# A DeltaNet and feed-forward kernel: the last 891 steps of a written-out order, arranged anew

## The chip, the cores and the metric

The kernel runs on one core of one Trainium2 chip. The metric is the time of one execution on the device in microseconds (us), the median of several runs.

## The reference

Two blocks stand one behind the other. The first goes through 768 tokens for each of 4 batches and 8 heads and carries a 48 x 48 state:

```python
k_n = k / (np.linalg.norm(k, axis=-1, keepdims=True) + 1e-06)
state = np.zeros((B, H, D, D), dtype=np.float32)
for t in range(S):
    kt, vt, bt = (k_n[:, :, t], v[:, :, t], beta[:, :, t, None])
    y[:, :, t] = np.einsum('bhd,bhde->bhe', q[:, :, t], state)
    v_old = np.einsum('bhde,bhd->bhe', state, kt)
    state = state + bt[:, :, :, None] * np.einsum('bhd,bhe->bhde', kt, vt - v_old)
```

The second takes the heads side by side as 3072 tokens of 384 features:

```python
a = x @ w1
b = x @ w2
h = a * b @ w3
return (h @ w_out).astype(np.float32)
```

w1 and w2 are 384 x 1024, w3 is 1024 x 1024, w_out is 1024 x 384, all in float32.

## The kernel before

The tokens are cut into 12 chunks of 64 (numbered m or c), and two chunks make a pair (j or u, 0 to 5). The token-by-token recurrence is replaced, in each chunk, by products of small matrices, for which a triangular matrix has to be inverted. The feed-forward block works on a pair of chunks at a time; w3 and w_out are first multiplied with each other into w34, and the last product is done with seven half-size products in place of eight (Winograd's form of Strassen).

Each part of the work is a Python generator, and each `yield` ends a step. `ORDER` names 1371 steps; a name stands in it once for each step of its generator, so the third "s4" is the third step of scores(4). The loop below runs them, and `in_text_order` ties every instruction to the one before it on its engine: the order of the text is the order on every engine's queue.

```python
    def step(name):
        if name not in running:
            running[name] = parts[name]()
        next(running[name], None)

    for name in ORDER.split():
        step(name)
    in_text_order()
```

In this document a name with a point, such as s4.0, means the first step of s4. The names that matter here:

- k, v, p: loads of one chunk (k: 4 DMAs on SP, v: 2, p: 8 in each of 2 steps, into `perm`); d: four VectorE transposes of `perm` into `KQ`.
- g (squares) and N (norms): lengths of the keys of a pair: POOL squares (L272), VectorE sums (L274), a tiny TensorE product (L257); N.0 is 15 small VectorE operations.
- s (scores): twice a TensorE step of 48 matmul instructions (L369, L375) and two VectorE steps that read its bank. u: 4 DMAs that carry the result to DRAM.
- V (inverse): loads a pair's triangles as 32 x 32 blocks and inverts them in 31 VectorE steps of a product and a subtraction (L442, L449), each needing the one before; then a DMA stores them. For the first two pairs V works in a PSUM bank.
- e (corner): 8 DMAs load the inverse, VectorE transposes it (L485), and two TensorE steps of 64 matmul instructions (L502) with ScalarE copies behind them (L518, L529) fill in the corner of the 64 x 64 inverse.
- n: POOL scales v. c (chain): three TensorE steps of 64 (L555), each followed by VectorE (R L588, X L598, the state S L619). y (outputs): one TensorE step of 128 (L656), ScalarE copies into `xT` (L677), and for odd chunks 6 DMAs within `xT`.
- P, C, t, f: weights loaded, converted (ScalarE L717, VectorE L722, POOL L724), transposed and folded into w34. C30 to C35 make w2s. T: sums of the folded weight on POOL (L840).
- a and b (ab): for pair u and slice jc, a product with w1s (6 matmul instructions, L791), a ScalarE copy (L803), a product with w2s (6, L791), and a VectorE product of the two (L807). The b steps are the first chunk of pair 0.
- S: 16 POOL sums of slabs (L860); o: seven products of 16 matmul instructions (L888); x (result): ScalarE and VectorE read the banks and SP stores the results.

PSUM is two tiles of two banks ("w", for s, e, c, y) and four banks ("f", for a, b, o, g, N), both given out in turn, so a TensorE step can wait until another engine has read what its bank held. A float32 matmul of the source is two matmul instructions in the profile. TensorE's own queue holds 8444 matmuls, as many weight loads, and 169 semaphore and drain instructions.

Of the kernel before, what the change touches and what calls it, by code (L numbers as in the profile page):

```python
# [52 lines left out]
f7 V1 V1 y0 b2 C31 b2 b5 V1 V1 P17 b3 V1 V1 V1 V1 V1 V1 V1 b5 b4 V1 V1 V1 c1 b6 V1 b6 y1 a05 b3  # L53
V1 V1 C31 V1 V1 C31 V1 b4 a01 a01 V1 V1 V1 a00 V1 V1 a05 a00 V1 V1 V1 C34 P16 V1 a06 b0 b7 a06
V1 b0 V1 V1 V1 V1 C32 C33 b7 p4 b1 V1 V1 V1 V1 C32 a07 V1 V1 a07 C34 a04 V1 V1 V1 V1 a04 V1 V1
V1 V1 V1 V1 V1 V1 V1 a02 V1 V1 k4 g2 V1 V1 b1 a03 d4 d4 a03 C32 C34 a00 b0 C33 C35 a02 a00 v3
k5 b1 n3 C35 b0 b1 a03 a03 g2 g2 b2 b2 g2 a01 C35 V1 b3 v2 c1 a01 C33 b3 b6 a07 n2 V1 b6 V1 g2
g2 p4 a06 g2 c2 g2 g2 d4 d4 e2 e2 e2 a04 e2 n2 a07 c2 a06 e2 s4 e2 T b4 g2 N2 s4 c2 s4 T a02 c2
c2 c2 y2 b4 p5 y2 b5 d5 s4 a04 e3 S0 V2 d5 a05 a02 o0 T N2 e3 n3 c3 a05 s4 s4 b5 T c3 S0 e3 p5
d5 d5 b7 b7 u4 e3 S0 S0 S0 S0 e3 s5 S0 k6 N2 x0 o0 S0 s5 e3 s5 s5 s5 u5 s5 c3 g3 o0 g3 c3 x0 y3  # L60
S0 y3 S0 g3 o0 o0 g3 V2 V2 x0 V2 c3 x0 V2 S0 S0 V2 V2 o0 V2 y3 V2 p6 x0 V2 S0 x0 S0 S0 V2 x0 x0
S0 V2 V2 V2 a10 a10 V2 v4 x0 o0 x0 x0 V2 d6 V2 d6 V2 a12 p6 V2 V2 a13 V2 V2 a12 a13 v5 V2 V2 V2
a14 a11 V2 V2 a17 a17 a14 k7 V2 g3 a14 n4 V2 V2 V2 V2 V2 a14 a17 a11 g3 g3 g3 V2 a13 a13 e4 d6
d6 a11 c3 a16 c4 n4 e4 e4 a17 a11 p7 c4 a16 a15 e4 g3 e4 e4 g3 e5 a15 a15 N3 s6 s6 s6 c4 e5 a12
c4 y4 d7 d7 a15 p7 a16 n5 n5 y4 a12 a16 c4 e5 c4 a10 a10 e5 S1 e5 e5 c5 o1 c5 S1 S1 k8 d7 x1 S1
S1 d7 s7 s7 s7 s7 S1 s7 s7 S1 S1 g4 g4 o1 v6 g4 s6 s6 s6 S1 u7 c5 o1 V3 c5 x1 y5 c5 u6 g4 V3 S1
c5 V3 V3 y5 x1 o1 o1 S1 S1 y5 c6 V3 S1 V3 p8 S1 n6 x1 S1 V3 V3 V3 V3 V3 o1 x1 V3 x1 S1 x1 a20
a20 o1 n6 V3 x1 V3 V3 V3 V3 a24 a24 x1 x1 a25 V3 a25 V3 a22 V3 V3 d8 k9 d8 V3 V3 V3 V3 a21 p8
a27 a27 a21 V3 V3 V3 V3 x1 V3 V3 a27 a22 V3 V3 v7 n7 V3 g4 e6 a20 a27 e7 d8 a23 d8 a23 g4 a24
a26 g4 g4 a20 a24 c6 N3 p9 n7 g4 S2 e6 g4 e6 a26 a26 N4 e6 s8 s8 e6 a25 N3 e7 e6 s8 a26 c6 c6  # L70
s8 N4 s8 s8 N4 y6 y6 d9 d9 e7 e7 a23 a21 a25 a23 c6 u8 c6 e7 p9 d9 a22 d9 V4 a22 e7 a21 S2 S2
s9 s9 c7 o2 s9 s9 S2 S2 c7 c7 s9 s9 S2 S2 c7 v8 S2 k10 o2 u9 g5 g5 V4 V4 S2 S2 x2 o2 x2 y7 o2
o2 V4 V4 V4 V4 y7 x2 S2 V4 c7 x2 V4 S2 V4 V4 S2 S2 y7 V4 o2 x2 x2 x2 x2 S2 a35 V4 V4 S2 V4 n8
V4 n8 V4 a35 x2 o2 x2 a37 V4 V4 V4 p10 x2 V4 V4 d10 a33 a33 d10 g5 V4 a34 a37 V4 g5 a30 a34 k11
a30 a36 V4 V4 p10 v9 a36 V4 a34 V4 V4 V4 a31 V4 a33 a30 V4 g5 V4 V4 e8 g5 a31 g5 g5 a33 a34 d10
a32 a32 e8 g5 e8 a30 V5 c7 a31 e8 e8 c8 a36 e8 e9 g5 e9 a31 d10 n9 c8 v11 c8 e9 p11 a37 c8 e9
e9 e9 c8 c8 N5 a36 a35 y8 n9 c9 d11 y8 a32 c9 c9 N5 a32 s10 a37 o3 a35 x3 o3 s10 d11 o3 c9 S3
s10 s10 s10 S3 p11 d11 d11 S3 x3 S3 S3 y9 y9 S3 S3 o3 S3 v10 s10 N5 s11 S3 s11 s11 S3 s11 S3 S3
x3 s11 o3 x3 u10 y9 u11 c9 s11 c9 o3 a47 x3 S3 S3 V5 x3 S3 n10 x3 x3 V5 S3 o3 V5 x3 x3 V5 V5 V5
a47 V5 V5 V5 V5 V5 V5 V5 a43 V5 a42 a43 a46 a46 V5 V5 a42 V5 a46 a40 x3 V5 n11 V5 a41 n11 V5 V5  # L80
a46 V5 V5 V5 a41 a40 V5 V5 V5 a47 a41 V5 V5 V5 a45 V5 V5 V5 a47 e10 a41 a40 a45 a44 e10 a43 a45
n10 e11 a40 c10 a43 a44 a45 e10 a44 c10 e10 e10 e11 e10 a42 a42 c10 o4 a44 S4 S4 S4 c10 e11 x4
S4 S4 c10 S4 e11 o4 S4 e11 c10 c11 S4 o4 c11 e11 c11 S4 c11 S4 y10 S4 y10 S4 y11 S4 x4 S4 o4 o4
y11 x4 x4 o4 x4 x4 y11 x4 a50 x4 x4 a50 S4 S4 o4 x4 a50 a55 a55 a50 a55 a51 a57 a51 a55 a51 a51
a54 a54 a56 a57 a52 a52 a52 a53 a56 a53 a56 a53 a52 a54 a57 a54 x4 a56 S5 S5 S5 a53 o5 a57 o5
S5 S5 x5 o5 x5 S5 S5 S5 S5 S5 o5 o5 S5 S5 x5 o5 S5 x5 S5 x5 S5 S5 o5 x5 x5 x5 x5 x5 x5 x5 x5 x5
"""


# [975 lines left out]
```

## Time and profile before

| | |
|---|---|
| median of 3 runs | 600.25 us (599.49 to 600.57) |
| the profiled execution | 601.93 us, span of its instructions 600.2 us |
| mean granted TensorE clock | 0.980 |
| TensorE busy | 542.4 us |
| VectorE, ScalarE, POOL busy | 329.7, 164.2, 173.6 us |
| DMA | 56.54 MB, mean 94 GB/s |

"Granted clock" is the share of TensorE's full clock. In the rows of the trace a wait stands in brackets with what ended it; "issue" means that the engine waited for nothing that the profile shows.

### The profile page before, as it was taken

The page shows a single profiled execution, that of the slowest core. Times are in us where ns is not written, and L with a number is a line of the kernel's source. Part 1 is how long each engine was busy: PE and PEld are TensorE (multiplying, and loading weights), DVE is VectorE, ACT ScalarE, POOL GpSimd, SP SyncE. Part 2 cuts the span into 40 slices and gives each one's busy share as a digit, 9 for nine tenths or more (in the row PEclk, how much of TensorE's full clock was granted, in tenths as well). Part 3 has the DMA queues.
Part 4 walks back from the last instruction along what each step waited for, and adds up shares of the span by engine and source line. Part 5 has one row for each costly group of instructions (what it writes and reads, how often), then busy time and mean ns, then how long its engine had stood idle before and what let it go on. Part 6 is the DMA issues. An engine that isn't in the chain of part 4 may idle for free.

```text
span 600.2 us, 19394 instructions
## 1 busy us (share of the span) xinstructions
PE 542.4 (90%) x8444; PEld 378.7 (63%) x8444; DVE 329.7 (55%) x788; ACT 164.2 (27%) x345; POOL 173.6 (29%) x222
## 2 busy tenths in 40 slices
PE   2378994889899999999999899999999999999997
PEld 2364663658678884558854569645588446884477
DVE  2457763457786379665696644975545963211012
ACT  3486653734312211131211312012310111320100
POOL 6364433230535700207203016021071001500051
PEclk9988996899999999999999989999999999999999
DMA  8959887596953356525546352463253021010001
GB/s 225 219 135 276 233 163 128 82 176 96 164 80 55 56 123 108 98 42 84 103 78 127 50 81 73 82 114 65 40 86 94 14 59 32 5 54 13 1 0 53
DMA packets 204404, 56.54 MB, mean 94 GB/s; under 512 B 193344, under 2 KB 199488, under 8 KB 202528
## 3 DMA queue, kind: packets, MB, share of 16 engines
q1 hardware_dynamic: 200128, 54.52, 46.4%
q10 hardware_dynamic: 4192, 0.79, 0.9%
q8 instruction: 66, 1.08, 0.8%
q14 instruction: 18, 0.15, 0.1%
HBM read 43.09 MB, written 11.01 MB: 90 GB/s over the span
## 4 chain that ended last, share of the span: by engine, by line
PE 80%; DMA 6%; issue 4%; DVE 4%; ACT 4%; SPq 1%; POOL 0%; ACTq 0%; DVEq 0%
PE ps_f L791 39%; PE ps_f L888 18%; PE ps_w L555 5%; PE ps_f L771 5%; PE ps_w L656 4%; DMA raw<-in_moe_w_dram 3%; PE ps_w L502 3%; PE ps_w L369 2%; PE ps_w L375 2%; DMA ktok<-in_k_dram 2%; DVE ps_w L449 1%; DVE tb L442 1%; DMA Vd<-Vb 1%; ACT raw L720 1%; PE ps_w L888 1%
## 5 line engine op out<-in xcount | busy, mean ns | idle before, releaser
L791 PE MATMUL ps_f<-xT,w2s 128*128 128x512 f32 (+1 forms) x336 | 134.2, 544 | 3.0 <-POOL w2s L724 2.8
L860 POOL TENSOR_TENSOR ab<-ab 128x256 f32<-128x256 f32 x96 | 66.8, 728 | 223.5 <-DVE ab L807 190.0
L791 PE MATMUL ps_f<-xT,w1s 128*128 128x512 f32 (+1 forms) x336 | 128.2, 532 | 0.3 <-issue 0.3
L791 PEld LDWEIGHTS ps_f<-xT,w2s 128*128 128x128 f32 x336 | 62.5, 191 | 57.9 <-issue 50.9
L791 PEld LDWEIGHTS ps_f<-xT,w1s 128*128 128x128 f32 x336 | 63.3, 190 | 55.8 <-issue 51.7
L803 ACT COPY ab<-ps_f 128x512 f32<-128x512 f32 (+1 forms) x56 | 27.9, 527 | 185.6 <-PE ps_f L791 185.6
L888 PE MATMUL ps_f<-w,ab 128*128 128x192 f32 x376 | 66.3, 330 | 0.0
L807 DVE TENSOR_TENSOR ab<-ab,ps_f 128x512 f32<-128x512 f32 (+1 forms) x56 | 32.9, 604 | 59.1 <-PE ps_f L791 58.5
L888 PEld LDWEIGHTS ps_f<-w,ab 128*128 128x128 f32 x376 | 61.2, 190 | 3.9 <-issue 2.7
L442 DVE TENSOR_TENSOR tb<-Vb,Ub 128x31 f32<-128x31 f32 (+15 forms) x124 | 43.9, 354 | 16.4 <-DMA Ub<-Ud 13.0
L771 PE MATMUL ps_f<-w2s,w3T 128*128 128x384 f32 x128 | 45.4, 507 | 4.9 <-ACT w3T L765 3.5
L888 PE MATMUL ps_f<-room,ab 128*128 128x192 f32 x272 | 48.0, 330 | 0.8 <-DVE room L919 0.8
L449 DVE TENSOR_TENSOR Vb<-Vb,tb 128x31 f32<-128x31 f32 (+15 forms) x124 | 44.6, 360 | 4.3
L888 PEld LDWEIGHTS ps_f<-room,ab 128*128 128x128 f32 x272 | 44.1, 190 | 1.6 <-issue 1.1
L677 ACT COPY xT<-ps_w 48x256 f32<-48x256 f32 x96 | 30.5, 366 | 49.1 <-PE ps_w L656 48.6
L272 POOL TENSOR_TENSOR sq<-ktok 128x384 f32<-128x384 f32 x24 | 20.2, 852 | 75.7 <-DVE tb L442 39.1
L381 DVE TENSOR_TENSOR U<-ps_w,wt 128x512 f32<-128x512 f32 x24 | 16.5, 689 | 42.6 <-PE ps_w L375 42.5
L771 PEld LDWEIGHTS ps_f<-w2s,w3T 128*128 128x128 f32 x128 | 24.2, 195 | 21.5 <-ACT w3T L765 4.0
L375 PE MATMUL ps_w<-KQ 48*64 48x64 f32 x768 | 29.4, 227 | 6.3 <-issue 4.7
L724 POOL TENSOR_TENSOR w<-w,raw 128x512 uint32<-128x512 uint32 x16 | 20.7, 1298 | 33.1 <-DVE w L722 15.7
L375 PEld LDWEIGHTS ps_w<-KQ 48*64 48x64 f32 x768 | 26.1, 140 | 5.6 <-issue 3.9
L541 POOL TENSOR_TENSOR vtok<-vtok,n 128x384 f32<-128x384 f32 x24 | 19.8, 838 | 33.3 <-DMA vtok<-in_v_dram 33.3
(104 smaller groups left out, 644.7 us busy)
## 6 DMA issues: line engine op xcount, KB each, us to landing
raw<-in_moe_w_dram SPq DMA_DIRECT2D x8, 1024.0 KB, 8.1
vtok<-in_v_dram SPq DMA_DIRECT2D x24, 192.0 KB, 4.5
raw<-in_moe_w_dram SPq DMA_DIRECT2D x12, 384.0 KB, 6.7
out_dram<-osb SPq DMA_DIRECT2D x46, 96.0 KB, 2.7
ktok<-in_k_dram SPq DMA_DIRECT2D x44, 96.0 KB, 3.5
raw<-in_moe_w_out_dram SPq DMA_DIRECT2D x4, 768.0 KB, 5.0
Ud<-U SPq DMA_DIRECT2D x48, 64.0 KB, 2.3
Ub<-Ud SPq DMA_DIRECT2D x6, 512.0 KB, 3.9
```

The lines of the kernel that those rows point to most:

```text
L375: pe.matmul(ps[half(z ^ j), 1, n + C * j : n + C * j + C], lhsT=x[:, 0, :], rhs=x[:, j, :], start=True, stop=True,)
L442: dve.tensor_tensor(out=tv, in0=V[:, 0 : s + 1, s : s + 1].to_broadcast([P, s + 1, n]), in1=U[:, s, s + 1 : BS].unsqueeze(1).to_broadcast( ...
L449: dve.tensor_tensor(out=o, in0=o, in1=tv, op=ALU.subtract)
L555: pe.matmul(out(ps, r, h, z), lhsT=lhs(r, h, z), rhs=rhs(r, h, z), start=True, stop=True,)
L656: i = pe.matmul(region(h, z, r), lhsT=lhs, rhs=rhs, start=part[n] not in part[:n], stop=part[n] not in part[n + 1 :],)
L677: act.copy(out=xT[f, p:NP:2, b : b + NR, cc, :].rearrange("p a r t -> p r a t"), in_=pyv[f, z, b : b + NR],)
L771: pe.matmul(ps[:, 0:DM], lhsT=w3Ts[jc, kc // 4][:, kc % 4 * P : kc % 4 * P + P], rhs=wo[:, kc], start=(kc == 0), stop=(kc == KF - 1),)
L791: pe.matmul(ps[:].rearrange("p b c t -> p b (c t)"), lhsT=w[:, m, js], rhs=x[:, m, :, c0:c1].rearrange("p b c t -> p b (c t)"), start=(m = ...
L803: act.copy(out=t, in_=ps)
L807: dve.tensor_tensor(out=t, in0=t, in1=ps, op=ALU.mult)
L860: pool.tensor_tensor(out=o_, in0=x_, in1=y_, op=op)
L888: pe.matmul(ps[b][:, b, :], lhsT=abs_[u, HF * f + i][:, t0 : t0 + P], rhs=ws_[w][:, i], start=first and i == 0 and (b == 0 or n == "F"), s ...
```

## The change

The first 480 steps keep their places. The 891 that follow are put in a new order, laid out with the exact places where TensorE's packets of instructions begin; no step is added or removed, and no other line of the kernel changes. In the profile TensorE is at 155 us, and VectorE and POOL at about 156 us, where the new order begins. The diff, cut to the places that the text speaks of:

```diff
-V1 V1 V1 V1 V1 V1 V1 a02 V1 V1 k4 g2 V1 V1 b1 a03 d4 d4 a03 C32 C34 a00 b0 C33 C35 a02 a00 v3
-k5 b1 n3 C35 b0 b1 a03 a03 g2 g2 b2 b2 g2 a01 C35 V1 b3 v2 c1 a01 C33 b3 b6 a07 n2 V1 b6 V1 g2
-g2 p4 a06 g2 c2 g2 g2 d4 d4 e2 e2 e2 a04 e2 n2 a07 c2 a06 e2 s4 e2 T b4 g2 N2 s4 c2 s4 T a02 c2
...
-S0 y3 S0 g3 o0 o0 g3 V2 V2 x0 V2 c3 x0 V2 S0 S0 V2 V2 o0 V2 y3 V2 p6 x0 V2 S0 x0 S0 S0 V2 x0 x0
-S0 V2 V2 V2 a10 a10 V2 v4 x0 o0 x0 x0 V2 d6 V2 d6 V2 a12 p6 V2 V2 a13 V2 V2 a12 a13 v5 V2 V2 V2
...
-s8 N4 s8 s8 N4 y6 y6 d9 d9 e7 e7 a23 a21 a25 a23 c6 u8 c6 e7 p9 d9 a22 d9 V4 a22 e7 a21 S2 S2
-s9 s9 c7 o2 s9 s9 S2 S2 c7 c7 s9 s9 S2 S2 c7 v8 S2 k10 o2 u9 g5 g5 V4 V4 S2 S2 x2 o2 x2 y7 o2
-o2 V4 V4 V4 V4 y7 x2 S2 V4 c7 x2 V4 S2 V4 V4 S2 S2 y7 V4 o2 x2 x2 x2 x2 S2 a35 V4 V4 S2 V4 n8
...
-S4 S4 c10 S4 e11 o4 S4 e11 c10 c11 S4 o4 c11 e11 c11 S4 c11 S4 y10 S4 y10 S4 y11 S4 x4 S4 o4 o4
-y11 x4 x4 o4 x4 x4 y11 x4 a50 x4 x4 a50 S4 S4 o4 x4 a50 a55 a55 a50 a55 a51 a57 a51 a55 a51 a51
...
+V1 V1 V1 V1 V1 V1 V1 a02 V1 V1 k4 v2 b1 C34 C32 V1 g2 d4 b1 V1 V1 C33 a03 k5 v3 b3 a02 b1 n2 n2
+a00 a00 a02 d4 V1 C35 C35 V1 a03 p4 b3 a01 g2 C33 a02 C35 b5 c1 b5 a01 a03 a07 e2 b6 g2 g2 g2
+g2 a06 b6 e3 a03 g2 g2 c2 n3 e2 e2 c2 a07 b4 a06 e2 e2 e2 T b4 a04 g2 c2 d4 d4 p5 g2 a04 c2 b0
...
+S0 S0 x0 S0 o0 S0 S0 s5 V2 V2 y3 x0 o0 c3 V2 V2 g3 x0 V2 y3 y3 V2 V2 V2 k7 S0 o0 x0 x0 V2 x0 x0
+x0 V2 V2 V2 V2 a13 o0 x0 p6 a17 V2 a17 V2 V2 V2 a15 V2 V2 a13 d6 a14 d6 a11 a11 V2 v4 p6 a16 V2
...
+a27 a22 v8 s8 a25 p9 y6 y6 S2 e7 a23 s8 e7 d9 d9 a25 c6 a23 S2 S2 o2 o2 S2 S2 e7 S2 S2 S2 S2 c6
+p9 d9 d9 e7 e7 S2 S2 S2 c7 s9 u8 c7 x2 o2 x2 c7 s9 s9 s9 s9 k10 s9 o2 p10 c7 u9 x2 y7 o2 x2 o2
+V4 V4 V4 V4 x2 c7 S2 S2 y7 y7 x2 d10 x2 S2 S2 a32 o2 x2 x2 a37 V4 V4 V4 k11 V4 V4 V4 a37 V4 x2
...
+y8 a35 o3 p11 d11 e9 S3 S3 a37 d11 c8 c8 e9 S3 S3 p11 S3 S3 g5 g5 x3 S3 o3 s10 n9 c9 N5 v10 c9
+o3 s10 s10 c9 s10 x3 n10 o3 S3 S3 c9 y9 y9 s10 u10 s10 x3 S3 y9 d11 S3 S3 d11 c9 c9 o3 s11 x3
...
+c10 e11 c10 o4 e11 S4 S4 S4 c11 x4 o4 e11 y10 y10 S4 c11 c11 c11 o4 o4 y11 x3 x4 x4 y11 x4 S4
+S4 y11 S4 S4 o4 x4 x4 x4 x4 x4 S4 S4 S4 S4 o4 x4 a51 a51 a52 a53 a53 a56 a56 a52 a51 a54 a50
...
```

## The prediction, made before the result was known

> **What bounds the kernel now.** I read the page first, then TensorE's own waits from 155 us on (the new order begins there: the last step that both orders share, the load k4, has its DMAs issued until 152.84 us, and TensorE's next common product ends at 153.88).
>
> ```profile
> PE 542.4 (90%) x8444; PEld 378.7 (63%) x8444; DVE 329.7 (55%) x788; ACT 164.2 (27%) x345; POOL 173.6 (29%) x222
> PEclk9988996899999999999999989999999999999999
> q8 instruction: 66, 1.08, 0.8%
> PE 80%; DMA 6%; issue 4%; DVE 4%; ACT 4%; SPq 1%; POOL 0%; ACTq 0%; DVEq 0%
> ```
>
> TensorE is 90% busy and carries 80% of the chain that ended last. The line to keep is q8: TensorE's program comes in 66 transfers of 16 KB, for 8444 matmuls and as many weight loads, so 256 instructions a packet, some 127 pairs. Its waits from 155 us on:
>
> ```profile
> PE ps_w L656 <- issue: 3.1, 4, 1.0
> PE ps_f L791 <- POOL w2s L724: 2.8, 2, 2.3
> PE ps_w L502 <- issue: 1.6, 1, 1.6
> PE ps_w L375 <- issue: 1.4, 1, 1.4
> PE ps_f L888 <- DVE room L919: 0.8, 1, 0.8
> PE ps_w L369 <- issue: 0.8, 1, 0.8
> PE ps_w L656 <- DVE X L598: 0.2, 1, 0.2
> ```
>
> Only the lines with POOL and DVE are waits for data. "Issue" means that TensorE waited for nothing the profile shows, and always at a line of small products (L369, L375, L502, L656). I counted TensorE's instructions ahead of each (matmuls, weight loads, and the 169 semaphore and drain instructions of its queue). The seven longest fall at the matmuls numbered 2245, 2499, 2880, 5163, 6559, 6940 and 8081, and all seven counts leave the same remainder by 256: these are the first instructions of packets. They lasted 0.80, 0.74, 1.36, 1.61, 0.58, 0.99 and 0.75 us, together 6.84. The trace's record of queue 8 gives the mechanism: before the 1.61 us wait the packet ahead had begun at 339.83, the next one's transfer ran from 340.94 to 342.22, and its first matmul started at 343.72. From one packet's start to the next took 3.89, 2.58, 4.81, 3.89, 3.85, 3.22 and 3.09 us in the seven cases, so a packet holding less TensorE work than about 3.4 to 3.9 us makes it wait. What followed the longest:
>
> ```profile
> 341.85 0.26 PE L502 MATMUL ps_w<-T,U 33*33 33x32 f32 x9
> 343.72 0.68 PE L502 MATMUL ps_w<-T,U 33*33 33x32 f32 x55 [1.61 <-issue]
> 344.33 4.97 PE L791 MATMUL ps_f<-xT,w2s 128*128 128x512 f32 x7
> ...
> 531.30 2.84 PE L888 MATMUL ps_f<-room,ab 128*128 128x192 f32 x16 [0.81 <-DVE room L919]
> ```
>
> ```profile
> 200.00:340.00 140.00, 139.42 (x2161) 92.06 (x2162) 96.69 (x238) 25.04 (x55) 32.14 (x45) 1.00 0.48 88
> 340.00:350.00 10.00, 8.29 (x192) 4.76 (x188) 3.20 (x7) 3.69 (x10) 0.00 (x0) 0.83 0.49 69
> ```
>
> The windows (length, then busy PE, PEld, DVE, ACT, POOL, then PEclk) show PE busy 139.4 of 140 us, and behind the 1.61 us wait a granted clock of 0.83: one stretch of 3.41 us at half clock, in which the six matmuls of a23's second product took 4.47 us where the same step behind small products takes 2.77.
>
> **The change part by part.** The steps are the same, so I take durations from this execution (601.93 us, span 600.2, against a median of 600.25) and apply differences to the median. Letters are steps of the order, and the number after the point is which step of it, from 0.
>
> *Packets, a gain of 6.0.* I laid TensorE's steps out in both orders with their counts (a product of ab 6 matmuls, o 16, a half of scores 48, each product of chain and corner 64, outputs 128, as many loads, and the semaphores that each step carried here) and their times (a 2.58, o 2.60, c 0.7 to 1.1, e 0.6 to 0.8, s 0.9 to 1.1, y 2.0 to 2.2), and cut every 256 instructions. The old order has packets of 2.83, 2.03, 3.10, 3.52, 3.47, 2.75, 2.42, 3.58, 3.13, 2.22, 2.87, 2.87 and 2.09 us. The two of 2.87 cost nothing: long o products lay ahead, behind which the transfer had started early. The new order has 3.21 (y6, a23), the same two of 2.87, a 2.75 that also follows two o products, then 3.73 and 3.89. The first is short of 3.85 by 0.6; with 0.2 for the others I leave 0.8 of 6.84. Bounds: 0.2, when only what lies under 3.4 counts; 1.9, when every shortfall below 3.8 (3.6 us in all) is paid at the old order's rate (6.84 for 12.5).
> The Trainium skill, "Runtime: NRT & Kernel Launch", section "Instruction fetch mechanics", says that the crossing of such a block is mostly hidden; the trace differs, 6.84 us at seven of them; by that rule this term would be nought.
>
> *Clock, a gain of 1.7* (4.47 less 2.77), as the wait ahead of it goes. The packet ahead of it had 2.42 of work; the two there now have 3.21 and 5.27.
> The Trainium skill, "TensorE: Matmul & The Clock Gate", section "HAM oscillation", would have no gap under 3.4 us throttle; here 1.61 us came before one; by that rule the term is nought.
>
> *The start, a gain of 2.1.* POOL at 155 us:
>
> ```profile
> 155.77 0.83 POOL L272 TENSOR_TENSOR sq<-ktok 128x384 f32<-128x384 f32 x1 [16.66 <-DMA ktok<-in_k_dram]
> 156.56 2.53 POOL L724 TENSOR_TENSOR w2s<-w2s,raw 128x512 uint32<-128x512 uint32 x2
> ```
>
> The two conversions that TensorE waited for (C32, C34) stood behind a square that waited 16.66 us for its tokens; VectorE's part of them had ended at 151.10. The new order has them ahead of it: 151.1 + 2 x 1.29 = 153.7, about when TensorE arrives. The old idle here was 2.83 in the waits and 0.54 in a product that stretched over them. Late next is C35: ScalarE now takes it behind V1's copies (ended 157.94), then 1.2 + 0.9 + 1.3 and a queue on each of VectorE and POOL, as before until about 162.6, while TensorE reaches b5's second product after six products of 1.29 from 153.9 and a 0.26 wait for a bank, at 161.9: 0.7. With 0.3 at e2, 1.3 remains of 3.4. Bounds: a gain of 1.0 to 3.0.
>
> *Adjacent o products, a loss of 1.35.* o's sixth product needs a bank that VectorE reads after the fifth. Where both stood side by side (o4, above) it cost 0.81. The new order parts that pair with y11 (a gain of 0.81), but sets o2.4 and o2.5 together (0.8), and o4.5 and o4.6, between which two VectorE operations of 0.55 must run: 0.81 + 0.55 = 1.36.
>
> *More alternation, a loss of 0.75.* A large product behind small ones takes 0.2 longer (a 2.77 for 2.58, o 2.80 for 2.60); there are 47 such places for 43. Bounds 0.4 and 1.0.
>
> *Thinner covers, a loss of 1.3 (0.5 to 2.5).* Ahead of c9.2, VectorE has from the end of c8.4 on 1.9 (c8.5), 0.4, 3.5 (norms N5), 0.95, 0.7 and 0.7, or 8.15 us, under 7.65 of TensorE work: 0.5. s9.0 takes the bank that ScalarE empties in 1.18 us (e7.5) under c7.0, 0.95: 0.3. o0.5, y2 and e3.4: 0.5 together. ab's first product of each pair needs outputs' copies and xT's DMAs behind them on SP: the traced need is 5.8 to 6.7 us from y's end, the new cover 6.5 for u=1, 7.1 for u=3 and 6.8 for u=5: nothing. The loads moved on SP (v2 ahead of k5; k7 ahead of x0's first VectorE store, 2.9 us of issue) have no reader closer than that.
>
> *The recurrence V, allowed 1.0 (0 to 3).* With its waits gone TensorE comes earlier to each e that needs V's result:
>
> ```profile
> 241.06 0.35 SPq L457 DMA_DIRECT2D Vd<-Vb  x1
> 247.88 0.71 DVE L485 STREAM_TRANSPOSE T<-TT 128x512 f32<-128x512 f32 x1
> 250.15 0.76 PE L502 MATMUL ps_w<-T,U 33*33 33x32 f32 x64
> ```
>
> From the end of o0's last product (223.50) VectorE and the DMAs needed until 248.60, 25.1 us. New, one more V step lies behind it (0.8): 25.9, under 26.9 us of TensorE work. Likewise V3: 25.4, and 0.8 for a V step, and 2.5 for c5's sum and a reduction that now stand ahead of V's end, less 2.9 as they no longer stand behind it, 25.8 under 27.2. V4: 23.3, five V steps (4.7), 1.1 of other work less, 26.9 under 29.5. V5: 30.2 and 0.9, 31.1 under 34.8. All are covered, the first two by 1.0 and 1.4 only.
>
> Sum: 6.0 + 1.7 + 2.1 less 1.35, 0.75, 1.3 and 1.0 is 5.4: **594.8**.
>
> **The rivals.** *Packets elsewhere*: the semaphore instructions of the new order are counted by the old one's. Displaced by 16 instructions, the shortfall below 3.4 us is 4.4 to 5.7 where it is 1.9 as laid (7.7 before). At 0.89 us for each (6.84 for 7.7), 2.8 more is paid: 597.6. For my count: the shortfall has its least value, among shifts of up to 64 either way, at no shift.
> *VectorE becomes the bound (slower)*: V3, V4 and V5 have 27.2, 30.9 and 26.5 us for the same 31 steps here, by what lies between. If each of the four chains runs longer by that spread, 4.4 us, they are late by 3.4, 3.0, 1.8 and 0.7, 8.9 us in place of the 1.0 allowed: 602.7. It decides from 3.8 us longer each (2.8 + 2.4 + 1.2, the 6.4 that the rest of the sum gains). For: slacks of 1.0 and 1.4. Against: the V steps keep their own durations.
> *The packets' places do not matter*: issue waits as before and the half clock too, 7.7 less gain: 602.5. Against: seven of seven on one remainder. The first rule of the Trainium skill quoted above would lead here.
> *The clock falls anyway*, at another wait, as it did at one of seven: 596.5. The second rule quoted above would lead here too.
>
> **How the numbers follow.** Forecast 0.62, packets elsewhere 0.14, VectorE 0.12, places that do not matter 0.07, the clock 0.05. About 0.2%, 1.2 us, is what a measurement can tell from no change. Faster: 0.58 of the forecast, 0.11 of the displaced packets, 0.05 and 0.01, 0.75. Same: 0.03 each of forecast, displaced and VectorE, 0.09. Slower: 0.16. The range runs from 592.0 (bounds: 0.2 for packets, 0.5 for covers, nothing for V) to 600.5, which takes in the displaced packets and the forecast's own worse bounds.
>
> **What would show it.** From 155 us on: issue waits of 1 us or less in all, the largest near y6 and a23; PEclk 1.00 in every window; PE busy with w2s before 155; 0.8 ahead of o2's sixth product and 1.4 ahead of o4's seventh; e4 and e6 unwaited. It is wrong if issue waits stay at several us, or if L502 waits for T or TT from VectorE.

## The result, and the profile after

The new order takes 593.8 us (median of 4 runs, 593.61 to 594.4), the old one 600.37 (4 runs, 599.49 to 600.57): a ratio of 0.9895, with a 95% interval of 0.9878 to 0.9912, 6.6 us less. The forecast was 594.8.

The profiled execution took 593.88 us, its span 592.2, 8.0 below the old one's 600.2. Not all of this belongs to the change: TensorE's last common product (a02.0) ended at 153.88 us before and at 153.19 now. What follows is therefore measured from there to TensorE's last matmul, a stretch that I call the tail part. It fell from 442.26 to 434.91 us, by 7.35: 5.50 in TensorE's idle time (11.98 to 6.48) and 1.85 in its busy time. Behind the last matmul both kernels need 4.1 us.

The page first, three of the lines shown of before:

```profile
PE 547.0 (92%) x8444; PEld 383.0 (65%) x8444; DVE 331.0 (56%) x788; ACT 164.0 (28%) x345; POOL 174.6 (29%) x222
PEclk9778995889999999999999999999999999999999
q8 instruction: 66, 1.08, 0.8%
```

The packets are as many as before; nothing was taken out of the program. The granted clock is at nine tenths or more from the tenth slice on; the low digits stand in slices ahead of the change. TensorE's busy time over the whole span rose from 542.4 to 547.0 us, all of it ahead of the tail part, where it fell. TensorE's waits from 150 us on (us in total, times, longest; all line numbers are one higher than before):

```profile
PE ps_f L889 <- DVE osb L920: 1.3, 1, 1.3
PE ps_w L370 <- DVE KQ L327: 1.3, 2, 1.0
PE ps_f L889 <- DVE room L920: 0.8, 1, 0.8
PE ps_f L792 <- issue: 0.7, 1, 0.7
PE ps_w L556 <- PE ps_f L889: 0.4, 1, 0.4
PE ps_w L370 <- ACT TT L530: 0.3, 1, 0.3
PE ps_w L503 <- ACT T L519: 0.2, 1, 0.2
```

No small product waits for "issue" any more. The one issue wait left, 0.66 us at 212.02, is not at a packet's first instruction: it stands ahead of a13's first product, 19 places from one, and two of the DMAs into xT, which that product reads, landed at 211.76 and 211.93, just ahead of its first weight load at 211.99. Every other line names data. The windows, and the two pairs of o products:

```profile
200.00:340.00 140.00, 138.02 (x2030) 87.15 (x2033) 98.35 (x236) 24.42 (x54) 27.40 (x38) 1.00 0.49 88
340.00:350.00 10.00, 9.88 (x277) 7.89 (x266) 5.14 (x8) 3.69 (x10) 3.93 (x6) 1.00 0.33 43
```

```profile
368.31 1.38 PE L889 MATMUL ps_f<-room,ab 128*128 128x192 f32 x7 [0.81 <-DVE room L920]
...
525.86 1.38 PE L889 MATMUL ps_f<-w,ab 128*128 128x192 f32 x7 [1.32 <-DVE osb L920]
```

The stretch at half clock is gone: 1.00 where it was 0.83. The stretch from 200 to 340 is a little less full than it was (138.0 for 139.4 of 140): data waits stand there now. And POOL at the start of the new order, with TensorE's first w2s product:

```profile
149.33 2.54 POOL L725 TENSOR_TENSOR w2s<-w2s,raw 128x512 uint32<-128x512 uint32 x2 [13.10 <-DVE w2s L723]
152.70 0.83 POOL L273 TENSOR_TENSOR sq<-ktok 128x384 f32<-128x384 f32 x1 [0.82 <-DMA ktok<-in_k_dram]
```

```profile
153.03 1.46 PE L792 MATMUL ps_f<-xT,w2s 128*128 128x256 f32 x6
```

The two conversions end at 151.9, the square comes behind them, and TensorE goes from w1s to w2s without a wait.

### The profile page after: what moved, and what is told of

Its sections match the earlier page's. It is cut to its first block, busy times and chain, and to the rows that moved or that the text cites. A ratio compares the mean times of both kernels' runs of the same rounds, so it can differ in the third digit from the quotient of the medians.

```text
span 592.2 us, 19395 instructions
## 1 busy us (share of the span) xinstructions
PE 547.0 (92%) x8444; PEld 383.0 (65%) x8444; DVE 331.0 (56%) x788; ACT 164.0 (28%) x345; POOL 174.6 (29%) x222
## 5 line engine op out<-in xcount | busy, mean ns | idle before, releaser
L792 PE MATMUL ps_f<-xT,w1s 128*128 128x512 f32 (+1 forms) x336 | 130.3, 542 | 0.8 <-issue 0.7
L792 PE MATMUL ps_f<-xT,w2s 128*128 128x512 f32 (+1 forms) x336 | 130.6, 537 | 0.0
L792 PEld LDWEIGHTS ps_f<-xT,w1s 128*128 128x128 f32 x336 | 64.8, 195 | 56.2 <-issue 51.4
L443 DVE TENSOR_TENSOR tb<-Vb,Ub 128x31 f32<-128x31 f32 (+15 forms) x124 | 45.5, 367 | 11.9 <-DMA Ub<-Ud 8.2
L370 PE MATMUL ps_w<-KQ 48*64 48x128 f32 x384 | 29.2, 293 | 1.9 <-DVE KQ L327 1.3
```

The costliest lines, as they stand in the source:

```text
L370: pe.matmul(ps[half(z), 0, n : n + 128], lhsT=x[:, 0, :], rhs=x.rearrange("p j t -> p (j t)"), start=True, stop=True,)
L443: dve.tensor_tensor(out=tv, in0=V[:, 0 : s + 1, s : s + 1].to_broadcast([P, s + 1, n]), in1=U[:, s, s + 1 : BS].unsqueeze(1).to_broadcast( ...
L792: pe.matmul(ps[:].rearrange("p b c t -> p b (c t)"), lhsT=w[:, m, js], rhs=x[:, m, :, c0:c1].rearrange("p b c t -> p b (c t)"), start=(m = ...
```

## The experiments

The theory: most of the gain comes from where packets begin, with the half clock behind one of those waits; the next part from POOL's conversions. The rival: the gain came from the order of the data, and the packets' places do not matter. In the experiments the first 150 us scattered from run to run (a02.0 ended between 147.6 and 156.9 us in the profiles), so the times scatter by several us and the tail part of the profiles is compared. Each kernel has one profile.

**e1, the new order with its packets displaced.** The tiny product of g2 (L257, four matmul instructions and as many loads for each pair of halves) writes the same result again:

```diff
-        for z in range(2):
+        for z in list(range(2)) * times:
...
-        yield from across(ss[:, 1], ss[:, 0])
+        yield from across(ss[:, 1], ss[:, 0], 13 if j == 2 else 1)
```

> The new order, with the tiny product that follows g2's sums written 12 more times onto its own result: 96 more instructions in TensorE's queue at about 170 us, which puts every later packet's first instruction 96 instructions earlier in the work. Packet theory: cut at these places, the new order has eight packets of 1.8 to 2.9 us of work, 5.7 us more shortfall below 3.4 us than as laid; 5 to 7 us of issue waits come back at first instructions of packets, perhaps with a stretch of half clock (1.7), and the 48 tiny matmuls cost about 1.3 themselves: 599 to 603 us against 593.8. Rival (the gain came from the order of the data, and the packets' places do not matter): the tiny matmuls alone, 595 us.

The median was 607.25 us, 1.0158 (1.0061 to 1.0255) of the old order's on that chip. TensorE's waits from 153 us on:

```profile
PE ps_w L556 <- issue: 2.4, 2, 1.5
PE ps_w L376 <- issue: 2.1, 2, 1.2
PE ps_w L503 <- issue: 1.9, 1, 1.9
PE ps_f L889 <- DVE osb L920: 1.3, 1, 1.3
PE ps_w L657 <- issue: 1.1, 1, 1.1
```

Six issue waits, 7.6 us together, and counted as in the prediction all six stand at a packet's first instruction. Two stretches of 3.41 us at half clock came with them, one straight behind the 1.95 us wait:

```profile
195.20 0.32 PE L503 MATMUL ps_w<-T,T 33*33 33x32 f32 x5 [1.95 <-issue]
195.44 4.43 PE L889 MATMUL ps_f<-room,ab 128*128 128x192 f32 x16
```

(o's product took 4.43 us for 2.8.) From the end of the tiny product to the last matmul the new order needed 415.1 us, this one 425.4. The data waits of 1.3, 0.8, 0.4 and 0.3 us are those of the new order, untouched. The rival's 595 us is out. The median lies above the 599 to 603 us that I expected: the waits came to 7.6 us for 5 to 7, and there were two stretches of half clock for one.

The record of queue 8 shows what these waits end with. In all 33 issue waits of over 0.15 us at packets' starts, in the tail parts of the old order, e1, e2, e4 and e9, TensorE's first matmul came 1.19 to 1.58 us after the end of a packet's transfer.

**e3, a whole packet more.** As e1, with 33 in place of 13: 256 more instructions.

> The new order with 32 more of the tiny product, 256 instructions, one whole packet: every later packet begins at the same work as in the new order. Packet theory: no issue wait at any packet's start after that, and only the cost of the 128 tiny matmuls, about 3.3 us: 596.5 to 597.5, and less than the kernel with 12 of them. Rival (it is the added instructions, not their number by 256, that disturb): more than the kernel with 12, some 600 us or above.

```profile
PE ps_f L889 <- DVE osb L920: 1.3, 1, 1.3
PE ps_f L889 <- DVE room L920: 1.0, 2, 0.8
PE ps_w L370 <- DVE KQ L327: 0.4, 1, 0.4
PE ps_w L556 <- PE ps_f L889: 0.4, 1, 0.4
```

No issue wait, although nearly three times as many instructions were added as in e1. What counts is the number by 256. The median was 597.74 (0.9961, 0.9923 to 0.9999), just above the 596.5 to 597.5 expected. The tiny product ran from 167.79 to 172.46 and so cost some 4.4 us more than in the new order, not 3.3. The clock was at half from 170.91 for 6.83 us: 1.55 of them fell on the tiny matmuls and the other 5.28 on the work behind. From the tiny product's end it took 415.2 us, the new order's 415.1, but this equality is luck: the half clock cost about 2.3 us there, and waits of the new order that did not occur in this run, ahead of a13 (0.66) and s7 (0.95) above all, gave as much back.

**e2, the old order with its packets displaced.** The same edit in the old order, 7 in place of 13: 48 instructions.

> The old order, with the same tiny product written 6 more times: every later packet begins 48 instructions earlier in the work, where my cutting of the old order shows 3.0 us less shortfall below 3.4 us (4.7 for 7.7). Packet theory: the issue waits after 172 us fall from 6.8 us to about 4, and the stretch of half clock behind the 1.61 us wait goes or moves; the tiny matmuls cost about 0.7: 596 to 598.5 us against 600.4. Rival (places do not matter): 601 us.

```profile
PE ps_w L555 <- issue: 1.5, 2, 1.1
PE ps_w L502 <- issue: 0.6, 1, 0.6
PE ps_w L656 <- issue: 0.5, 1, 0.5
```

The median was 596.87 us, 0.9951 (0.9908 to 0.9994). The issue waits at packets fell from 6.84 to 2.62 us (0.60, 1.10, 0.38 and 0.54), no half clock followed, and from the tiny product's end to the last matmul it took 417.2 us for 423.5: 6.2 us less with the order of every step untouched.

**e4, the old order with the conversions first.**

```diff
-k4 g2 V1 V1 b1 a03 d4 d4 a03 C32 C34 a00
+k4 C32 C34 g2 V1 V1 b1 a03 d4 d4 a03 a00
```

> The old order with one part of the new: POOL's two conversions C32 and C34 stand ahead of g2's first square and no longer behind its wait for tokens. Theory: TensorE's waits of 2.29 and 0.54 us at w2s and the stretched product behind them (0.5) go; C35 and the corner e2 then come due earlier and take back up to 1: 2.3 to 3.4 us less, 597 to 598 us against 600.4. Rival (the recurrence V or the loads hold the next stage anyway, as e2's transpose waited for its turn until 171.4 us): all of it is given back at e2, 600 us.

```profile
153.49 2.75 PE L791 MATMUL ps_f<-xT,w2s 128*128 128x256 f32 x12
```

The time settles nothing: 599.8 us, 0.9998 (0.9951 to 1.0045), where I expected 597 to 598. The trace does. The w2s waits are gone, and from a02.0's end to the start of g2's tiny product it took 15.1 us for 18.5, 3.4 less; from its end to the last matmul it took 422.0 for 423.5, so nothing was given back at e2 or behind. The issue waits stayed, 6.2 us, all eight at packets' first instructions.

**e8, the new order with the conversions last again.**

```diff
-k4 v2 b1 C34 C32 V1 g2 d4
+k4 v2 b1 V1 g2 C34 C32 d4
```

> The new order with one part undone: the conversions C34 and C32 stand behind g2's first square again, which waits for its tokens until about 155.8 us. Theory: TensorE's first w2s product (b1), reached at about 153.2, waits until C34 ends at 157.9 and so 3 to 4.5 us; the stages behind have slack of 1.0 or more only, so nearly all of it reaches the end: 3 to 4.5 us more from 153 us to the end. Rival (V and the loads hold the next stage, and TensorE only waits here rather than there): less than 1.5 us reaches the end.

```profile
156.48 1.13 PE L792 MATMUL ps_f<-xT,w2s 128*128 128x256 f32 x4 [2.79 <-POOL w2s L725]
```

One wait of 2.79 us, and half clock behind it from 157.7 to 161.1. The tail part took 438.5 us, 3.6 more than the new order's 434.9: the wait and about 1.7 of half clock (six matmuls took 2.54 us for 1.46, the next twelve 3.41 for some 2.75), less 0.9 elsewhere. The median was 597.48 where e5 to e7 on the same chip had 593.3 to 593.7. The rival (less than 1.5 us arrives) is out.

**e9, the old order with both edits**, e4's and e2's.

> The old order with two small edits only: POOL's conversions C32 and C34 ahead of g2's first square, and the tiny product behind g2's sums written 6 more times (48 instructions of TensorE's queue). If the start (3.4 us) and the packets' places (6.2 us from g2's tiny product to the end, measured in the kernel with the second edit alone) add up, TensorE needs 432.5 to 434 us from a02's end to its last matmul, as few as in the new order (434.9) where the old one took 442.3. Rival (the two gains are one: with the start gone the packets' waits come back at other places, or V holds the stages): 437 us or more.

**e10, the new order once more**, on the same chip:

> The new order as it is, beside the others on this chip: 434 to 435.5 us from a02's end to the last matmul, no issue wait at a packet's start; s7's wait of 0.95 us for the load p7 and a13's of 0.66 vary from run to run if the DMA queues cause them.

TensorE's issue waits in e9, the kernel with the two edits, from 150 us on:

```profile
PE ps_w L656 <- issue: 2.2, 3, 1.1
PE ps_w L555 <- issue: 1.6, 3, 0.8
PE ps_w L502 <- issue: 1.1, 1, 1.1
PE ps_w L375 <- issue: 0.7, 1, 0.7
```

The new order repeated its tail part (434.94), without an issue wait at a packet's start. The two edits took 436.6, short of the 432.5 to 434 that I expected and just below the rival's 437: the start was gained in full, but the waits at packets, cut at the same places as in e2, came to 5.7 us in this run, at eight packets, and not 2.6 at four. My count (4.7 us of shortfall at 0.89) had said 4.2, and the two runs lie on both sides of it. So the place sets which packets can be short, and whether and how long TensorE waits at one differs from run to run. In time the two are alike: 594.27 (0.9889, 0.9846 to 0.9932) for the two edits, 593.58 (0.9884, 0.9841 to 0.9928) for the new order.

**e5, two covers mended.** In the new order c7's last product goes between o2's fifth and sixth, and e7's second product between o2's first and second:

```diff
-c6 a23 S2 S2 o2 o2 S2 S2 e7 S2 S2 S2 S2 c6 p9 d9 d9 e7 e7 S2
+c6 a23 e7 S2 S2 o2 e7 o2 S2 S2 e7 S2 S2 S2 S2 c6 p9 d9 d9 S2
...
-y7 o2 x2 o2 V4 V4 V4 V4 x2 c7 S2
+y7 o2 c7 x2 o2 V4 V4 V4 V4 x2 S2
```

> The new order with two pairs parted: c7's last product stands between o2's fifth and sixth, and e7's second corner product between o2's first and second. If the 0.81 us ahead of o2's sixth product and the 0.29 ahead of s9 are waits for one VectorE read and one ScalarE copy, as priced, both go and nothing comes in their place: 1.1 us less TensorE idle after 155 us. Rival (a neighbour comes due instead, as the packets move by a few instructions): 0.3 us or less is gained.

Both waits went (0.81 and 0.29), and 0.45 us came in their place, ahead of pair 3's first product at 369.6, which now stands nearer to xT's DMAs. That is 0.65 less, between the theory's 1.1 and the rival's 0.3. The tail part took 434.0 us; the median was 593.67 (0.9877, 0.9807 to 0.9948).

**e6, one sum earlier.** In x4 the sum of M1 and bank C is formed a step sooner:

```diff
         plus("M1", "B")(ws_["U2"])
+        if u == 4:
+            plus("M1", "C")(ws_["W"])
...
-        yield from store(u, 1, 1, plus("U3", "C"))
+        yield from store(u, 1, 1, plus("W", "B") if u == 4 else plus("U3", "C"))
```

> The new order with the result step x4 changed: the sum of M1 and bank C is formed one step earlier (one more VectorE operation of 0.55 us), so that o4's last product waits no longer for two VectorE operations in a row behind the product ahead of it. If 1.32 us ahead of that product is these two operations, it falls to 0 to 0.1; o4's sixth, which waits for the operation ahead of the new one, stays unwaited under y11: 1.2 to 1.3 us less idle. Rival (ab's first product, behind xT's DMAs, takes it over, since y11 is no further away): 0.5 to 1 us of wait moves to a51.

The 1.32 us went, so it was the two VectorE operations, and the rival had its share:

```profile
530.34 4.10 PE L792 MATMUL ps_f<-xT,w1s 128*128 128x512 f32 x9 [0.59 <-DMA xT<-xT]
```

0.59 us of it is now a wait for xT. The tail part took 433.6 us, the median was 593.31 (0.9856, 0.9788 to 0.9925).

**e7, all three**, with g5's tiny product and its copies a step earlier:

```diff
-d11 c8 c8 e9 S3 S3 p11 S3 S3 g5 g5 x3
+d11 g5 c8 g5 c8 e9 S3 S3 p11 S3 S3 x3
```

> Both of these changes, and g5's tiny product and its copies one step earlier, ahead of c8's state sum, so that c9's second product has VectorE's reads 0.4 us sooner. If the three waits are independent: idle of TensorE after 155 us 2.5 to 2.8 us below the new order's, some 591 us where the new order has 593.8. Rival (each wait hides another): 1.5 us or less.

The tail part took 431.6 us, 3.3 below the new order's, and c9's wait fell from 0.39 to 0.18; the median was 593.26 (0.9864, 0.9792 to 0.9936), where I expected 591. Not all of the 3.3 is the edits' work. They took away 2.6 us of waits, and 1.3 came back ahead of two products that read xT (0.89 for 0.14, and 0.59). Another 1.9 is waits that the edits do not touch and that did not occur in this run (s7's 0.95, a13's 0.66, s5's 0.31). So the edits are worth about 1.3 us here, and the rival (1.5 or less) fits better than independent waits. Beside the new order on one chip:

> The new order with the three covers mended, again, beside the new order on one chip: 431.5 to 433 us from a02's end, and a median 2 to 3.5 us below the new order's; if the early part of the kernel scatters by more than this from run to run, the intervals of the two ratios overlap all the same.

It took 433.1 us for 434.9, and a median of 592.38 (0.9871, 0.9836 to 0.9906) for 593.58 (0.9884), 1.2 us less where I expected 2 to 3.5. The intervals overlap: in time this version is not told apart from the new order, in the trace it is 1.9 us shorter on this chip.

**e12, d7's transposes side by side.** s7's wait of 0.95 us, which the prediction did not have, is left. VectorE runs d7's two last transposes with a16's product and a read of s6 between them:

```diff
-a10 s6 d7 a16 s6 d7 s6 u6
+a10 s6 d7 d7 a16 s6 s6 u6
```

> The new order with the three covers mended, and the two last transposes of d7 side by side on VectorE: in the new order a16's product and one of s6's reads (1.2 us) stand between them, and s7's first product waited 0.95, 0.69 and 1.0 us in three runs. If those two operations are the wait, it goes: 0.7 to 1 us less idle than with the covers alone, 430.5 to 432.5 us from a02's end to the last matmul. Rival (the load p7 lands late, whatever VectorE's order): s7 still waits 0.3 us or more.

s7 waits no longer. Of TensorE's waits from 152 us on, the longest is xT's:

```profile
PE ps_f L792 <- DMA xT<-xT: 0.6, 1, 0.6
PE ps_w L370 <- DVE KQ L327: 0.4, 1, 0.4
```

The tail part took 431.4 us, the shortest of all, though only 0.15 below e7's; the median was 592.78 (0.9898, 0.9843 to 0.9953). The second line is s5's. But e1, e3 and e7 had shown no wait at s7 either, while it was 0.30 to 1.0 us in e5, e6, e8, e10 and e11. VectorE's own wait tells these runs apart. Here are d7's two last transposes in the new order, and below them in e12:

```profile
269.46 0.71 DVE L327 STREAM_TRANSPOSE KQ<-perm 128x512 f32<-128x512 f32 x1 [4.31 <-DMA perm<-in_q_dram]
271.27 0.69 DVE L327 STREAM_TRANSPOSE KQ<-perm 128x512 f32<-128x512 f32 x1
...
267.35 1.31 DVE L327 STREAM_TRANSPOSE KQ<-perm 128x512 f32<-128x512 f32 x2 [3.66 <-DMA perm<-in_q_dram]
```

The first of them waits for p7's load. In the six runs in which s7 waited (the new order, e5, e6, e8, e10, e11), its wait was this one less 3.36 us, within 0.01; in e1, e3 and e7 VectorE had waited 3.36 or less. In e12 it waited 3.66, as in e8, where s7 then waited 0.30, and s7 did not wait. So p7's landing sets the size of s7's wait, and the edit took away 0.30 us of it in this run; more than that it had no occasion to show.

## Why the prediction was right, point by point

The tail part fell by 7.35 us in the profile and the median by 6.6; the sum had said 5.4. The steps:

- *Packets*: 6.84 us of issue waits, of which I left 0.8. None is left. The packet that I counted as short (y6 and a23, 3.21 of work) went by without a wait, although only 2.26 us lay between its first instruction (339.66) and the next packet's (341.92). The next packet's transfer had started at 338.63, while the long product ahead, a25's, was still running; I had made that allowance for o products and not for a25's. e1 to e3 show that the place by 256 is the cause. This also settles the rivals "packets elsewhere" (the count held) and "places do not matter". The Trainium skill ("Runtime: NRT & Kernel Launch", section "Instruction fetch mechanics") calls a crossing mostly hidden. By count the traces agree, as 44 of 51 packets in the old tail part began without a wait of over 0.15 us; but the other seven cost 6.84 us there, and six cost 7.6 us in e1, so the term was not nought.
- *Clock*, 1.7 forecast: a23's second product took 2.84 us for 4.54 (from its first matmul's start to its last one's end in both), and no stretch at half clock fell into the tail part.
- *The start*, 2.1 forecast: the old idle there (2.83, and 0.54 in the stretched product) went entirely, 3.4, as e4 also measured. Mis-sized was what comes due next: C35's conversion and e2 cost nothing in the first profile and at most 0.8 us in e10 (waits of 0.37 and 0.43 among the w2s products, the second for POOL's conversion), not 1.3.
- *Adjacent o products*: 0.8 and 1.36 forecast, 0.81 and 1.32 measured; the price of one pair in the old trace carried over to the others.
- *Thin covers*: c9.2 0.39 for 0.5, s9.0 0.29 for 0.3, e3 0.18, and s5 0.31, which I had not priced; o0.5 did not wait. *Alternation*: busy time without the clock's 1.7 and the stretch's 0.54 rose by 0.4, for 0.75.
- *The recurrence V*, allowed 1.0: no e waited for it, so the rival in which VectorE becomes the bound is out. The transposed blocks of e4, e6, e8 and e10 stood ready 2.5, 1.2, 1.4 and 1.1 us before TensorE took them, where I had worked out 1.0, 1.4, 2.6 and 3.7: covered as forecast, but the last by much less.
- *Missed*: two waits. s7's 0.95 (I had said that no moved load has a close reader; p7 has one in d7's transposes) and xT's, 0.66 ahead of a13 and 0.14 ahead of a32, where I had a cover of 6.5 against a need of 5.8 to 6.7 and called it nothing. The copies and DMAs took longer here: the six issues 4.82 us for 3.75.

What was too small in the gains (0.8 and 1.3), the allowance for V (1.0), and what covers and alternation were charged too much (0.5) make 3.6; the two missed waits take back 1.75. That is 1.85 of the 1.95 between 5.4 and 7.35. The steps were right; that the total came within 1.0 us of the forecast is in part luck, as errors of both signs met. One sum of the range is also off: the three bounds named for its lower end give 592.4, and 592.0 comes out only with alternation's lower bound of 0.4 as well.

## What to carry to other kernels

Where TensorE runs hundreds of tiny matmuls between large ones, count its instructions by 256 and look at what lies between two such places: here a stretch with less than some 3.5 us of work often waited for the next packet, unless a large product had still been running when that packet's transfer began (2.26 us went by so). A reordering, or even 48 added instructions, moves these places. An "issue" wait that always falls on the same remainder comes from the packets and not from data. And price a new neighbour by the same pair elsewhere in the old trace: the waits that were worked out so came within about 0.1 us.

## What the runs showed of the hardware that I had not expected

- A stretch of 3.41 us at half clock began within 1.2 us behind gaps of 1.61 (the old order), 1.89 (e4), 1.95 (e1) and 2.79 us (e8), and of 0.88 in e1; none followed others of 2.29 (the old order), 1.49 and 1.17 us (e1). What makes the difference is not shown. The Trainium skill, "TensorE: Matmul & The Clock Gate", section "HAM oscillation", names gaps over about 3.4 us; here the measurement decides.
- 128 tiny matmuls in a row (e3) ran into 6.83 us of half clock although TensorE was never idle there.
- The same cut cost 2.6 us of waits in one run and 5.7 in another (e2, e9).
